# Second half's layer norm: transposing x on TensorE, or loading it already turned and spreading the scales by DMA

## Chip, cores and metric

One core of one Trainium2 chip runs the whole program. The metric is device time in microseconds, the median of the runs shown below. Engines are called as in the profile: PE (TensorE matmul), PEld (its weight load), DVE (VectorE), ACT (ScalarE), POOL (GpSimd) and SP (SyncE, which issues most transfers).

## What is computed

A transformer block on one sequence of 2048 tokens with 1024 features, in float32: an attention part and an MLP part, each behind layer norms and each added to its input.

```
x = A_x
h = x + _A_ref(_layernorm(x), wq, wk, wv, wo, beta)      # attention, 32 heads, 4 segments of 512 tokens, with a running memory
h2 = h + _B_ref(_layernorm(h), w1, b1, w2, b2)           # _B_ref normalises again, then 1024 -> 3584 -> gelu -> 1024

def _layernorm(x, axis=-1, eps=1e-5):
    m = jnp.mean(x, axis=axis, keepdims=True)
    v = jnp.var(x, axis=axis, keepdims=True)
    return (x - m) / jnp.sqrt(v + eps)
```

The change concerns the very first `_layernorm(x)`, and of it only the tokens 1024 to 2047.

## The kernel before

The tokens are worked in two halves of 1024, and a half in two slices of 512 (`sl` 0 and 1). Each half runs attention, the output product, the second layer norm, and the first MLP product (class `Mixer`). After both halves comes the second MLP product. So the first layer norm of the second half is needed when the mixer of the first half ends, and it is computed beside that mixer, in gaps.

**Precision.** Nearly every product is done three times on split operands. An operand is an upper part (`h`, a cast to the matmul type, made on ACT) and a lower part (`l`, the float32 value minus the upper part, made on DVE or POOL). `mm3` and `product` issue upper·upper, upper·lower, lower·upper. So every input of PE costs an ACT cast and a subtraction.

**Layer norm, `ln1`.** For four blocks of 128 tokens: load the block (tokens on partitions, tile `xt`), two `bn_stats` and one `bn_aggr` on DVE, three tiny operations on POOL (`v`, power, `nb`), one normalising ACT operation on 128x1024, and then eight 128x128 transposes on PE into two PSUM banks, two ACT casts (`yh`) and two DVE subtractions (`yl`). The result has features on partitions, as the q, k, v products want it. `ln1` is a generator. Each `yield` is one step, and `interleave(main, side, ratio)` runs `ratio` side steps for each main step. The four steps of one `product` are four main steps, 3 matmuls each.

**The mixer, `pair(j)`, j = 0 to 13.** It is a fast-matrix-product scheme with five products of 12 matmuls per pair. Combined weights S1 to S4 of two weight blocks (`r1`, `r2`) are added on POOL (`combine`, tiles `s`), then split by `made` (ACT cast, DVE subtraction, tiles `sa` or `sb`). For a pair j, PE runs in this order:

1. S1·T1 into `dps`,
2. S3·T3 into `bps`,
3. S2·T2 of the *next* pair into its own `bps` (`sixth(j + 1)`), whose S2 is made during this pair,
4. A22·T4, added into this pair's `bps`,
5. S4·B22, added into `dps`.

DVE drains after each: `u3` (reads `bps` after product 2), a sum with `dps`, `u2` (after product 3), and the two `ht` sums (after 4 and 5). Product 4 writes the bank that `u3` reads, so it can't start before `u3` is done. `combine(j + 2)` stands near the end of pair j in program order. In program order `made` for pair j+1 stands in pair j.

**Order.** Each engine works through its own instructions in program order. In the mixer and in attention the program order is kept by hand (`in_order`). `dps` and the transposes of `ln1` share the two PSUM banks tagged `pt`. Tiles tagged `ln` (four buffers) hold `xt`.

**Attention of the second half** starts with the products `kps`, `qps`, `vps` of unit 0 (8 steps of 3 matmuls each). `side` is there the split k and q; copied by DMA into `ks` and `qs`, they feed the first logits matmul `pqk`.

## Time and profile before

| what | value |
|---|---|
| runs | 2184.59 us median of 3 (2183.11 to 2187.11) |
| profiled execution | 2187.23 us, of which the profile's span is 2185.5 us |
| PE busy | 2157.7 us, 99% of the span |
| DVE, ACT, POOL busy | 1349.0, 1102.1, 959.7 us (62%, 50%, 44%) |
| granted clock of PE | 1.000 |
| part in question | about 710 to 880 us: mixer pairs 5 to 13 of the first half, then the first two attention units of the second |

A profile line such as `712.89 0.72 ACT L1031 ACTIVATE ht<-ht,b1c ...` reads: start in us, duration in us, engine, line of the kernel, operation, output and inputs by the program's tile names, and how many instructions were merged. In square brackets stands how long the engine sat idle before it, and what ended that. A matmul's duration overlaps that of its neighbours, since matmuls are pipelined. What a matmul costs is the distance from its start to the next start.

### The profile page before, as it was taken

How to read it: one execution, taken by the hardware profiler on the slowest of the kernel's cores; microseconds unless marked ns; L12 is line 12 of the kernel's file. 1: busy time of each engine (PE TensorE's matmuls, PEld its weight loads, DVE VectorE, ACT ScalarE, POOL GpSimd, SP SyncE). 2: the span in 40 equal slices, each digit the busy share in tenths (PEclk: the TensorE clock that was granted, in tenths of full speed). 3: DMA queues.
4: the chain of work that ended last, by engine and by line, in shares of the span. 5: the costliest groups of instructions: out<-in, count | busy, mean ns of one | idle time of the engine just before them, and what ended most of it. 6: DMA issues, size and time to landing. Idle time of an engine off the chain costs nothing.

```text
span 2185.5 us, 33210 instructions
## 1 busy us (share of the span) xinstructions
PE 2157.7 (99%) x10937; PEld 1750.4 (80%) x10937; DVE 1349.0 (62%) x2696; ACT 1102.1 (50%) x2433; POOL 959.7 (44%) x1206
## 2 busy tenths in 40 slices
PE   7999999999999999999999999999999999999999
PEld 6777777778888888877777768888887888888887
DVE  6766666665745556766667655745666665576653
ACT  5777777762543445777777752643443232322221
POOL 5534345562444434533335561534446544256330
PEclk9999999999999999999999999999999999999999
DMA  6544445664465655544444663575569865676762
GB/s 182 134 106 107 105 107 136 190 203 164 154 207 155 187 158 147 136 107 109 106 108 133 198 197 141 173 217 162 171 199 373 274 226 185 190 244 230 250 222 92
DMA packets 352405, 376.20 MB, mean 172 GB/s; under 512 B 27214, under 2 KB 244330, under 8 KB 352234
## 3 DMA queue, kind: packets, MB, share of 16 engines
q1 hardware_dynamic: 288778, 336.98, 50.7%
q10 hardware_dynamic: 63456, 37.10, 5.6%
q8 instruction: 87, 1.43, 0.3%
q14 instruction: 84, 0.69, 0.1%
HBM read 241.27 MB, written 82.38 MB: 148 GB/s over the span
## 4 chain that ended last, share of the span: by engine, by line
PE 91%; DVE 2%; DMA 2%; POOL 2%; ACT 1%; issue 1%; SPq 0%; ACTq 0%; DVEq 0%; POOLq 0%
PE po L1410 22%; PE bps L1014 10%; PE cps L1014 7%; PE dps L1014 7%; PE pst L619 4%; PE po L633 3%; PE pqk L569 3%; PE kps L127 3%; PE vps L127 3%; PE qps L127 3%; PE kps L128 3%; PE pwo L127 2%; PE kps L129 2%; PE vps L128 2%; PE pwo L129 2%; PE pwo L128 2%
## 5 line engine op out<-in xcount | busy, mean ns | idle before, releaser
L571 DVE CUSTOM_DVE_ANT_0 pqk<-pqk,mask 128x512 f32<-128x512 f32 (+2 forms) x384 | 216.9, 565 | 241.6 <-PE pqk L569 214.8
L573 ACT ACTIVATE junk<-pqk,mx 128x512 f32<-128x512 f32 (+2 forms) x384 | 225.2, 587 | 134.7 <-DVE mx L571 128.2
L626 POOL TENSOR_SCALAR_AFFINE_SELECT e<-e 128x128 f32<-128x128 f32 (+1 forms) x384 | 137.6, 359 | 268.9 <-ACT e L622 254.1
L699 POOL TENSOR_TENSOR wl<-wr,wh 128x256 fp32r<-128x256 f32 x268 | 202.1, 770 | 108.7 <-PE pqk L569 85.8
L622 ACT ACTIVATE e<-pst 128x384 f32<-128x384 f32 (+1 forms) x384 | 200.8, 529 | 70.9 <-PE pst L619 69.5
L1420 DVE TENSOR_TENSOR c<-c,po 128x512 f32<-128x512 f32 x160 | 105.4, 684 | 156.7 <-PE po L1410 153.9
L569 PE MATMUL pqk<-ks,qs 96*128 96x512 f32 (+2 forms) x384 | 138.6, 361 | 5.7 <-ACT junk L573 3.0
L619 PE MATMUL pst<-qs,ks 104*128 104x512 f32 (+3 forms) x512 | 140.9, 318 | 1.0 <-ACT e L622 0.4
L619 PEld LDWEIGHTS pst<-qs,ks 104*128 104x128 f32 x512 | 95.7, 188 | 34.7 <-ACT e L622 10.7
L1410 PE MATMUL po<-w2h,zh 128*128 128x512 f32 x378 | 120.9, 389 | 0.4 <-DVE zh L1350 0.4
L1267 POOL TENSOR_TENSOR w2r<-w2r 128x512 f32<-128x512 f32 x54 | 84.6, 1579 | 72.3 <-DMA w2r<-in_B_w 72.3
L127 PE MATMUL kps<-yh,wh 128*128 128x512 f32 (+1 forms) x264 | 113.5, 430 | 0.0
L127 PE MATMUL qps<-yh,wh 128*128 128x512 f32 x256 | 113.2, 442 | 0.0
L1014 PE MATMUL bps<-zh,sb 128*128 128x512 f32 x336 | 110.9, 391 | 0.0
L1014 PE MATMUL bps<-zh,sa 128*128 128x512 f32 x336 | 110.8, 390 | 0.0
L1126 POOL TENSOR_TENSOR s<-r 128x512 f32<-128x512 f32 x28 | 44.3, 1583 | 141.0 <-DVE sa L1142 81.3
L127 PE MATMUL vps<-yh,wh 128*128 128x512 f32 x256 | 105.0, 410 | 0.0
L1410 PE MATMUL po<-w2h,hl 128*128 128x512 f32 x322 | 103.2, 390 | 0.7 <-DVE hl L1350 0.4
L128 PE MATMUL kps<-yl,wh 128*128 128x512 f32 (+1 forms) x264 | 102.8, 389 | 0.5 <-DVE yl L165 0.4
L129 PE MATMUL kps<-yh,wl 128*128 128x512 f32 (+1 forms) x264 | 102.2, 387 | 0.0
L128 PE MATMUL qps<-yl,wh 128*128 128x512 f32 x256 | 101.0, 394 | 0.0
L128 PE MATMUL vps<-yl,wh 128*128 128x512 f32 x256 | 100.8, 394 | 0.0
(271 smaller groups left out, 6204.0 us busy)
## 6 DMA issues: line engine op xcount, KB each, us to landing
hr<-h_dram SPq DMA_DIRECT2D x112, 448.0 KB, 5.5
w2r<-in_B_w SPq DMA_DIRECT2D x122, 256.0 KB, 4.2
r<-in_B_w SPq DMA_DIRECT2D x56, 512.0 KB, 4.6
ks<-kk SPq DMA_DIRECT2D x360, 64.0 KB, 2.0
qs<-qq SPq DMA_DIRECT2D x360, 64.0 KB, 2.0
h_dram<-ht ACTq DMA_DIRECT2D x84, 256.0 KB, 3.6
wx<-in_B_w SPq DMA_DIRECT2D x56, 256.0 KB, 3.5
o_dram<-side SPq DMA_DIRECT2D x52, 256.0 KB, 4.2
```

The source lines that it names most:

```text
L127: nc.tensor.matmul(ps, ah, bh, start=first, stop=False)
L128: nc.tensor.matmul(ps, ah, bl, start=False, stop=False)
L129: acts["mm"] = nc.tensor.matmul(ps, al, bh, start=False, stop=last)
L569: nc.tensor.matmul(ps, u["qs"][0:96, j, i * P:(i + 1) * P], u["ks"][0:96, j, 0:n], start=True, stop=True)
L571: nc.vector.tensor_tensor_reduce(out=ps, in0=ps, in1=mask[:, 512 - n:512], op0=ALU.add, op1=ALU.min, scale=-SCALE, scalar=3.0e38, accum_out=m)
L573: at(now[0] + 1, lambda: nc.scalar.activation(acts["junk"][:, :n], ps, AF.Exp, bias=m, scale=-1.0, accum_out=u["mx"][:, 1, i, j:j + 1]))
L619: nc.tensor.matmul(ps[:, o:o + 512 - P * jk], u["ks"][:, j, jk * P:(jk + 1) * P], u["qs"][:, j, jk * P:512], start=True, stop=True)
L622: nc.scalar.activation(e, ps[:, :w], AF.Exp, scale=SCALE)
L626: nc.gpsimd.affine_select(d, d, pattern=[[0, 2], [1, P]] if n == 2 else [[1, P]], compare_op=ALU.is_ge, fill=0.0, base=0, channel_multipli ...
L699: nc.gpsimd.tensor_tensor(l[:, c], wr[:, c], raw(h)[:, c], op=ALU.subtract)
L1014: nc.tensor.matmul(ps, x_[:, c, :], y_[:, c, :], start=first and c == 0 and n == 0, stop=last and c == 3 and n == 2, skip_group_check=True)
L1410: nc.tensor.matmul(ps, x_[:, k], y_[k], start=opens and k == 0 and i == 0, stop=closes and k == self.KP - 1 and i == 2, skip_group_check=True)
```

## The change

The host hands the kernel a second copy of x, transposed (`A_xT`, 1024 features by 2048 tokens). A new class `Columns` replaces `ln1` for the second half:

- `load` and `stats`: as before, the token blocks are loaded and their statistics taken on DVE and POOL. The results 1/std and -mean/std of four blocks lie side by side in `rn` (128 x 8).
- `turn`, `keep`, `spread`: one PE transpose makes `rn` into 8 rows of 128, ACT copies them to `rt`, a 4 KB DMA stores them in DRAM, and a second DMA reads them back onto all 128 partitions as `rows` (128 x 2 x 512).
- `columns`: four loads of 256 features by 512 tokens of `A_xT` (tile `xc`).
- `apply`: DVE multiplies `xc` by the row of 1/std (128x1024), POOL adds the row of -mean/std (128x1024).
- `upper`, `lower`: ACT casts to `yh`, DVE subtracts to `yl`, 128x1024 each, from SBUF and not from PSUM.

All steps of both slices up to `spread` lie in the last nine mixer pairs, at hand-set steps and with ratio 0.21 in place of 0.17. The `apply` steps of slice 1 lie in attention unit 0 (before, slice 1 ran on through units 0 and 1).

```diff
+    class Columns:
+        def load(self, t):
+            self.xs[t] = lnp.tile([P, D], F32, tag="ln", name="xt", bufs=4)
+            nc.sync.dma_start(self.xs[t], x[0, r0:r0 + P, :])
...
+        def stats(self, t):
+            for i in range(2):
+                nc.vector.bn_stats(st[:, i, :], self.xs[t][:, 512 * i:512 * i + 512])
+            nc.vector.bn_aggr(mv, st)
+            r = rn[:, t:t + 1]
+            nc.gpsimd.tensor_scalar(v[:, 0:1], mv[:, 1:2], 1.0, EPS, op0=ALU.mult, op1=ALU.add)
+            nc.gpsimd.tensor_tensor(r, v[:, 0:1], mhalf, op=ALU.pow)
+            nc.gpsimd.tensor_scalar(rn[:, 4 + t:5 + t], mv[:, 0:1], -1.0, r, op0=ALU.mult, op1=ALU.mult)
+
+        def turn(self):
+            ps = psum.tile([P, 512], F32, tag="av", name="prn", bufs=1)[0:8, 0:P]
+            nc.tensor.transpose(ps, self.rn, ident)
+            self.rt = acts["rnp"].tile([P, P], F32, name="rt", bufs=1)[0:8, :]
+            nc.scalar.copy(self.rt, ps)
+
+        def keep(self):
+            nc.sync.dma_start(rn_dram[self.half, self.sl], self.rt)
+
+        def spread(self):
+            self.rows = acts["rnp"].tile([P, 2, 512], F32, name="rows", bufs=1)
+            nc.sync.dma_start(self.rows.rearrange("p a n -> p (a n)"),
+                              rn_dram[self.half, self.sl].rearrange("k p -> (k p)").partition_broadcast(P))
+
+        def columns(self, c):
+            self.ws[c] = w = lnp.tile([P, 2, 512], F32, tag="ln", name="xc", bufs=4)
+            nc.sync.dma_start(w, xt_[256 * c:256 * c + 256, t0:t0 + 512].rearrange("(c p) n -> p c n", p=P))
+
+        def apply(self, c):
+            w = self.ws[c]
+            r, nb = (self.rows[:, i, :].unsqueeze(1).to_broadcast([P, 2, 512]) for i in range(2))
+            nc.vector.tensor_tensor(w, w, r, op=ALU.mult)
+            nc.gpsimd.tensor_tensor(w, w, nb, op=ALU.add)
...
+        def upper(self, c):
+            nc.scalar.copy(self.home(0, c), self.ws[c])
+
+        def lower(self, c):
+            nc.vector.tensor_tensor(self.home(1, c), self.ws[c], raw(self.home(0, c)), op=ALU.subtract)
+
+        def columns_at(self, *steps, lag):
+            for c, m in enumerate(steps):
+                self.at(m, partial(self.apply, c))
+                self.at(m + lag, partial(self.upper, c))
+                self.at(m + lag + 1, partial(self.lower, c))
...
-            acts["ahead"] = ln1(1, 1, gap=2)
-            interleave(chain(*(mixer.pair(j) for j in range(HP - 9, HP))),
-                       chain(ln1(1, 0, 2), islice(acts["ahead"], 3)), 0.17)
+            acts["rnp"] = tc.alloc_tile_pool(name="rn1", bufs=1, reuse_waits="tile")
+            one, two = Columns(1, 0), Columns(1, 1)
+            for t in range(4):
+                one.at(0, partial(one.load, t))
+                one.at(6 + t, partial(one.columns, t))
+                two.at(20 + 2 * t, partial(two.load, t))
+                two.at(26 + 2 * t, partial(two.columns, t))
+            one.rows_at(3, 4, 5, 6, turn=9, keep=10, spread=12)
+            one.columns_at(15, 17, 19, 21, lag=3)
+            two.rows_at(23, 25, 27, 29, turn=32, keep=33, spread=35)
+            interleave(chain(*(mixer.pair(j) for j in range(HP - 9, HP))), steps(one, two), 0.21)
+            two.columns_at(1, 3, 5, 7, lag=3)
+            acts["ahead"] = steps(two)
...
+    inputs = {**inputs, "A_xT": np.asarray(inputs["A_x"])[0].T}
```

Where the instructions then stand is shown at three places. The first is POOL's order in the mixer, pairs 9 and 10. `s` are the four sums of a `combine`; the sums s_8266 to s_8269 before, and s_8271 to s_8274 now, are those that pair 10 casts. Before:

```order
L1129 TENSOR_TENSOR s_8149<-r_8053,s_8147 128x512
L1126 TENSOR_TENSOR s_8266<-r_8177 128x512
L1127 TENSOR_TENSOR s_8267<-s_8266,r_8176 128x512
L1128 TENSOR_TENSOR s_8268<-r_8176,r_8177 128x512
L1129 TENSOR_TENSOR s_8269<-r_8176,s_8267 128x512
L141 TENSOR_SCALAR v<-mv 128x1
L142 TENSOR_TENSOR v<-v,mhalf 128x1
L147 TENSOR_SCALAR nb<-mv,v 128x1
L1126 TENSOR_TENSOR s_8389<-r_8301 128x512
```

The same place now:

```order
L1217 TENSOR_TENSOR s_8158<-r_8071,s_8156 128x512
L283 TENSOR_TENSOR xc<-xc,rows 128x1024 x3
L1214 TENSOR_TENSOR s_8271<-r_8182 128x512
L1215 TENSOR_TENSOR s_8272<-s_8271,r_8181 128x512
L1216 TENSOR_TENSOR s_8273<-r_8181,r_8182 128x512
L1217 TENSOR_TENSOR s_8274<-r_8181,s_8272 128x512
L283 TENSOR_TENSOR xc<-xc,rows 128x1024
L256 TENSOR_SCALAR v<-mv 128x1
L257 TENSOR_TENSOR rn<-v,mhalf 128x1
L258 TENSOR_SCALAR rn<-mv,rn 128x1
L1214 TENSOR_TENSOR s_8396<-r_8296 128x512
```

Three 128x1024 additions of slice 0 now stand on POOL ahead of one `combine`, and a fourth with the small operations ahead of the next one.

The second place is DVE from the end of pair 9 to `u3` of pair 10 (`sa`, `sb`: lower parts of the weights; the last row of each list is `u3`). Before:

```order
L165 TENSOR_TENSOR yl_7951<-pt,yh_7950 128x4x128
L1038 TENSOR_TENSOR ht<-bps,p1r 128x512
L134 BN_STATS st<-xt 128x6 x2
L138 BN_AGGR mv<-st 128x2
L1038 TENSOR_TENSOR ht<-dps,u_8122 128x512
L1142 TENSOR_TENSOR sb<-s_8267,sb 128x512
L1142 TENSOR_TENSOR sb<-s_8266,sb 128x512
L1142 TENSOR_TENSOR sb<-s_8268,sb 128x512
L1169 TENSOR_TENSOR u_8341<-bps,p1r 128x512
```

The same place now:

```order
L294 TENSOR_TENSOR yl_8239<-xc,yh_8238 128x1024
L282 TENSOR_TENSOR xc<-xc,rows 128x1024
L1126 TENSOR_TENSOR ht<-bps,p1r 128x512
L1126 TENSOR_TENSOR ht<-dps,u_8131 128x512
L1230 TENSOR_TENSOR sb<-s_8272,sb 128x512
L1230 TENSOR_TENSOR sb<-s_8271,sb 128x512
L1230 TENSOR_TENSOR sb<-s_8273,sb 128x512
L294 TENSOR_TENSOR yl_8239<-xc,yh_8238 128x1024
L282 TENSOR_TENSOR xc<-xc,rows 128x1024
L1257 TENSOR_TENSOR u_8341<-bps,p1r 128x512
```

A `lower` and a multiply of 128x1024 now stand between the weights' lower parts and `u3`. The multiply ahead of the `ht` sums of pair 9 is the one that the third of the three POOL additions waits for.

The third place is DVE at the start of the second half's attention, from the lower part of k to that of q (`side`). Before:

```order
L440 TENSOR_TENSOR side<-kps,side 128x512
L682 CAST ks_8733<-pat 8x2048
L165 TENSOR_TENSOR yl_8801<-pt,yh_8800 128x4x128
L382 SCALAR_TENSOR_TENSOR pk,zc<-e,r 128x512
L165 TENSOR_TENSOR yl_8801<-pt,yh_8800 128x4x128
L682 CAST ks_8734<-pat 8x2048
L134 BN_STATS st<-xt 128x6 x2
L138 BN_AGGR mv<-st 128x2
L440 TENSOR_TENSOR side<-qps,side 128x512
```

The same place now:

```order
L528 TENSOR_TENSOR side<-kps,side 128x512
L770 CAST ks_8747<-pat 8x2048
L294 TENSOR_TENSOR yl_8824<-xc,yh_8823 128x1024
L282 TENSOR_TENSOR xc<-xc,rows 128x1024
L470 SCALAR_TENSOR_TENSOR pk,zc<-e,r 128x512
L770 CAST ks_8748<-pat 8x2048
L294 TENSOR_TENSOR yl_8824<-xc,yh_8823 128x1024
L282 TENSOR_TENSOR xc<-xc,rows 128x1024
L528 TENSOR_TENSOR side<-qps,side 128x512
```

Two `lower` and two multiplies of 128x1024 stand where two 128x512 subtractions and one block's statistics stood.

## Prediction

> **What bounds the kernel now.** The page first, then the waits of PE alone in the part that changes (690 to 920 us; columns: who waited for whom, us in total, times, longest).

> ```profile
> span 2185.5 us, 33210 instructions
> PE 2157.7 (99%) x10937; PEld 1750.4 (80%) x10937; DVE 1349.0 (62%) x2696; ACT 1102.1 (50%) x2433; POOL 959.7 (44%) x1206
> ...
> PE dps L1014 <- DVE ht L1038: 0.9, 1, 0.9
> PE pqk L569 <- ACT junk L573: 0.8, 1, 0.8
> ```

> PE is the bound everywhere: two waits in 230 us. So each PE instruction removed is worth its distance in PE's stream, and each new wait of PE costs its full length. Next the tile `xt` from 700 us on, and PE's timeline about one group of transposes and about the first wait.

> ```profile
> L161 PE MATMUL pt<-ident,xt x64: 270/272/273, 740.5 to 878.4; 128*128 128x128 f32 x64
> ...
> 854.89 0.39 PE L129 MATMUL vps<-yh,wl 128*128 128x512 f32 x1
> 855.12 0.60 PE L161 MATMUL pt<-ident,xt 128*128 128x128 f32 x4
> 855.47 0.48 PE L127 MATMUL kps<-yh,wh 128*128 128x512 f32 x1
> 855.78 0.39 PE L128 MATMUL kps<-yl,wh 128*128 128x512 f32 x1
> ...
> 810.35 0.39 PE L1014 MATMUL dps<-zh,sb 128*128 128x512 f32 x1
> 811.61 0.47 PE L1014 MATMUL dps<-zh,sa 128*128 128x512 f32 x1 [0.88 <-DVE ht L1038]
> ```

> A 512-column matmul keeps a distance of 0.23 (854.89 to 855.12). With a group of four transposes, the matmul after L127 starts 0.66 after 855.12 and not 0.23. A group costs 0.43, not the 1.09 that four durations of 272 ns suggest.

> Now one undisturbed mixer pair (j = 5) on DVE, ACT and POOL. Zero is the `ht` sum at 712.17; the next pair's is 13.6 later.

> ```profile
> 712.17 0.69 DVE L1038 TENSOR_TENSOR ht<-dps,u 128x512 f32<-128x512 f32 x1 [2.03 <-PE dps L1014]
> 714.71 2.99 DVE L1142 TENSOR_TENSOR sa<-s,sa 128x512 fp32r<-128x512 f32 x3 [1.85 <-ACT sa L1141]
> 717.62 0.68 DVE L1169 TENSOR_TENSOR u<-bps,p1r 128x512 f32<-128x512 f32 x1
> 720.33 0.69 DVE L1156 TENSOR_TENSOR u<-bps,p1r 128x512 f32<-128x512 f32 x1 [1.30 <-PE bps L1014]
> 725.77 0.69 DVE L1038 TENSOR_TENSOR ht<-dps,u 128x512 f32<-128x512 f32 x1 [0.59 <-DMA r<-in_B_w]
> ...
> 712.89 0.72 ACT L1031 ACTIVATE ht<-ht,b1c 128x512 f32<-128x512 f32 x1 [2.00 <-DVE ht L1038]
> 714.05 1.67 ACT L1141 CAST sa<-s 128x512 fp32r<-128x512 f32 x3 [0.44 <-ACT ht L1031]
> 719.06 0.72 ACT L1031 ACTIVATE u<-u,b1c 128x512 f32<-128x512 f32 x1 [3.34 <-DVE u L1038]
> ...
> 715.53 1.61 POOL L1126 TENSOR_TENSOR s<-r 128x512 f32<-128x512 f32 x1 [5.48 <-DVE sa L1142]
> 717.23 1.63 POOL L1127 TENSOR_TENSOR s<-s,r 128x512 f32<-128x512 f32 x1
> ```

> Offsets in the pair: gelu 0.7, casts of S2, S1, S3 from 1.9, their lower parts 2.5 to 5.5, `u3` 5.5 to 6.1, `u2` 8.2. A product is 12 matmuls, 2.72 us. `u2` starts 0.2 after its product's successor did, so product 4 starts at 8.0, and product 3 at 5.3. The slack: S2's lower part is wanted at 5.7 (third matmul) and is there by 3.5; `u3` must end by 8.0 and ends at 6.1, 1.8 spare. POOL adds S1 and S2 for the *next* pair at 3.4 to 6.7, about 9 us before ACT casts them. That lead is what holds the mixer together, and it exists since nothing stands ahead of `combine` on POOL.

> **The change part by part.** *PE.* 64 transposes go: 16 groups by 0.43 = 6.9 off. Two transposes of `rn` come: a lone one between 0 and a group's 0.43; I take 0.1 each, since four share the 0.43. The wait at 811.61 goes: `dps` found its `pt` bank still held (1.26 from start to start, less 0.23: 1.0), and no transpose takes a `pt` bank any more. The 0.8 of `pqk` on ACT I leave as it is (bounds: 0 to 1.0 off). So far -7.7.

> *New elementwise work.* The nearest rows of its size, and the statistics, which stay:

> ```profile
> L926 DVE TENSOR_TENSOR hb<-ht,b2c x16: 1172/1210/1227, 510.5 to 1377.7; 128x1024 f32<-128x1024 f32 x16
> L104 POOL TENSOR_TENSOR wl<-wr,wh x2: 2401/2406/2411, 832.9 to 835.6; 128x1024 fp32r<-128x1024 f32 x2
> 834.52 1.04 ACT L103 CAST wh<-wr 128x1024 fp32r<-128x1024 f32 x1
> 723.65 1.28 DVE L134 BATCH_NORM_STATS2 st<-xt 128x6 f32<-128x512 f32 x2
> 724.97 0.21 DVE L138 BATCH_NORM_AGGREGATE mv<-st 128x2 f32<-128x12 f32 x1
> 781.61 0.19 POOL L141 TENSOR_SCALAR v<-mv 128x1 f32<-128x1 f32 x1 [1.61 <-DVE mv L138]
> 782.54 0.27 POOL L147 TENSOR_SCALAR nb<-mv,v 128x1 f32<-128x1 f32 x1
> ```

> So a multiply or a `lower` costs DVE 1.2, an addition POOL 2.4, an `upper` ACT 1.0, a block's statistics DVE 1.4 and then POOL 1.2. On average there is room (DVE 62% busy). The order is what matters, so I walk pairs 9 to 12 by these rows and the instruction order shown above.

> - *Pair 9.* First multiply of the pair after S3's lower part, at 4.4 to 5.7 (POOL idle, so the three take 1.9); `u3` ends 6.3, still in time. gelu of u 7.0 to 7.8, 0.4 of issue, then `upper` 8.2 to 9.2 ahead of the casts of A22 and S4 (to 10.3); their lower parts end 11.0, `lower` 12.2, the third multiply 13.4. POOL's third addition runs 13.4 to 15.8, that is until 2.2 in pair 10, and only then may `combine` start: S1 to 3.5, S2 to 4.8, S3 to 6.1. It had a lead of 9 us and now comes 3 late.
> - *Pair 10.* Cast of S2 4.9 to 5.5, S1 to 6.0, an `upper` to 7.0, S3 to 7.6. On DVE S3's lower part ends 8.3, then a `lower` 9.5, a multiply 10.7, `u3` 11.4. PE loses about 1.1 at product 3 and has waited 3.4 in all (11.4 less 8.0) when product 4 starts. The pair takes 17.0. Late on DVE after that: `u2`, A22, S4 (16.1), a `lower` (17.3), a block's statistics (18.7), and POOL's 1.2 for them: the next `combine` starts at 19.9, 2.9 into pair 11.
> - *Pair 11.* S2 is summed at 5.5. ACT, with an `upper` between the two gelus, casts it at 5.8 too. S2's and S1's lower parts end 8.1, a `lower` 9.3, statistics 10.7, S3 11.4, `u3` 12.1. PE waits 4.1.
> - *Pair 12.* The same chain with no `lower` in it: `combine` from 0.7, `u3` ends 8.5, 0.5 to 0.6 late.

> Sum in the mixer +8.1. Bounds: 0 if the lead of 9 us covers it all after all, 12 if DVE is slowed by POOL throughout. I take the walk, since each link is a row and the order is fixed. Slice 0's earlier statistics, also ahead of a `combine`, fit: in the same walk `u3` of pair 7 ends at 6.5.

> *Transfers.* Eight `xc` loads of 512 KB (the `r` loads' size) come, two `rows` spreads and two 4 KB stores, all on SP's queue, and what is behind a waiting one there is the next `r`.

> ```profile
> 820.00:840.00 20.00, 20.00 (x90) 16.57 (x89) 10.05 (x17) 6.81 (x9) 6.57 (x7) 1.00 0.49 144
> ```

> The DMA engines are half idle (0.49), and a pair's `r` is wanted only by the `combine` at its end. I cost them at 0; if that cover went, `combine` would start later still. The allocation of 4.6 KB a partition I cost at 0 too.

> *Attention unit 0.* Zero is `kps`' first matmul.

> ```profile
> 836.66 0.39 PE L127 MATMUL kps<-yh,wh 128*128 128x512 f32 x1
> 854.20 0.39 PE L569 MATMUL pqk<-ks,qs 96*128 96x512 f32 x1
> ...
> 844.48 0.69 DVE L440 TENSOR_TENSOR side<-kps,side 128x512 fp32r<-128x512 f32 x1 [5.44 <-ACT side L434]
> 847.24 0.68 DVE L382 SCALAR_TENSOR_TENSOR pk<-e,r 128x512 f32<-128x512 f32 x1
> 848.55 1.22 DVE L682 CAST ks<-pat 8x2048 fp32r<-8x2048 f32 x1
> 851.24 0.64 DVE L440 TENSOR_TENSOR side<-qps,side 128x512 fp32r<-128x512 f32 x1
> ...
> 849.31 3.10 SPq L417 DMA_DIRECT2D qs<-side  x3
> DMA to landing us min/median/max: 2.0/2.2/3.7
> ```

> `pqk` has no slack today: q's lower part ends at 851.9, its copy lands 2.0 later, 853.9, and `pqk` starts at 854.2 (17.5). Without the three groups ahead of it PE is there at 16.2. DVE's chain from the lower part of k (ends 8.5) becomes 1.2 + 1.2 + 1.2 + 0.7 + 1.2 + 1.2 + 1.2 = 8.0, so q's lower part ends at 17.1, not 15.2, and lands at 19.1. PE waits 3.1 with the weight load (bounds 1.0, nothing later than today, to 4.6). The third `pqk` then waits for its bank, as DVE has two `lower` more to do first: 0.7 (0 to 1.5). Later DVE and ACT have less to do than before, but PE hardly waits there.

> Sum: -6.9 + 0.2 - 1.0 + 8.1 + 3.1 + 0.7 = +4.2. The profiled execution took 2187.2 (2185.5 of span and 1.7 around it), 2.6 above the median 2184.6. So 2191.4 for such an execution, and 2188.8 against the median.

> [...] Three lower parts took 2.99 while POOL was adding. With POOL idle:

> ```profile
> 756.48 1.90 DVE L1142 TENSOR_TENSOR sb<-s,sb 128x512 fp32r<-128x512 f32 x3 [1.85 <-ACT sb L1141]
> ```

> `u3`, which reads PSUM, kept its 0.68 beside an addition. [...] By the rows, four more such meetings (two multiplies beside POOL's weight splits at the end of the mixer, and `lower` and `pk` beside the additions in unit 0) would add 4 by 1.1 = 4.4.

> **Rivals.**
> - *The cover holds, faster.* POOL's lead would have to absorb the additions, so that `u3` stays in time. For it: 9 us of lead and DVE half idle. Against it: the third addition waits for a multiply that can't end before 13.4. Time: -7.7 and the 1.0 floor of `pqk`, 2177.9. It decides on the multiply ending by about 8 in pair 9.
> - *Only the first stall is paid*, pairs 11 and 12 recover since the statistics come earlier than walked: -7.7 + 3.4 + 1.0, 2181.3.
> - *DVE and POOL get in each other's way*, by the rows above: 2188.8 + 4.4 = 2193.2, slower.

> **How the numbers follow.** The walk 0.60 (own range 2185 to 2193), cover 0.18, first stall only 0.10, contention 0.12. About 0.2% (4.4 us) is what a measurement of this kernel can tell from no change: below 2180.2 is faster, above 2189.0 slower. The walk's centre lies at that upper edge, so it is split, a little under half above: same 0.32, slower 0.28. Faster: 0.18 + 0.02 = 0.20; same: 0.32 + 0.08 = 0.40; slower: 0.28 + 0.12 = 0.40. The range takes in both outer cases: 2177.5 to 2195.5.

> **What the next profile would show.** No L161-like transposes after 40 us but two small `prn`. New rows of PE `bps` waiting for DVE `u`, some 2 to 3 us each in pairs 10 and 11, the pairs 17 long. POOL's first sum of that `combine` following an `xc` addition. `pqk` waiting for DMA `qs` about 3 us. Wrong I would be if PE has no such rows (gain 7), or if DVE's 128x1024 rows are far from 1.2.

## The result, and the profile after

The changed kernel takes 2198.58 us (median of 6 runs, 2195.89 to 2201.0), the kernel before 2185.38 (6 runs): ratio 1.0059, 95% interval 1.0045 to 1.0073. It is 13.2 us slower. The forecast was 2188.8 in a range up to 2195.5, so the time lies beyond the range on its slow side. The profiled execution after took 2197.16 (1.4 under its median), that of before 2187.2 (1.8 over its median), so the two spans differ by only 9.9.

First the two longest entries among the waits of PE alone from 690 to 920 us, kernel after, columns as in the prediction:

```profile
PE pqk L657 <- issue: 6.9, 1, 6.9
PE bps L1102 <- DVE u L1257: 5.5, 2, 2.9
```

Two waits for `u3` in the mixer, as forecast, and one of 6.9 at the first `pqk`, where 3.1 was forecast. In the kernel after, L282 is the multiply, L283 the addition, L294 the lower part, L256 a statistic's small operation, L1214 to L1217 `combine`, L1230 the lower parts of S1 to S4, L1257 `u3`, L528 the lower parts of k and q, L770 the pattern cast, L104 and L787 the weight splits. The mixer's pair 10, whose zero is now 779.60, on the timeline of the kernel after:

```profile
779.15 2.43 POOL L283 TENSOR_TENSOR xc<-xc,rows 128x1024 f32<-128x1024 f32 x1 [5.28 <-DVE xc L282]
781.54 1.29 POOL L1214 TENSOR_TENSOR s<-r 128x512 f32<-128x512 f32 x1
...
784.89 3.41 DVE L1230 TENSOR_TENSOR sb<-s,sb 128x512 fp32r<-128x512 f32 x3 [4.62 <-ACT sb L1229]
788.23 1.21 DVE L294 TENSOR_TENSOR yl<-xc,yh 128x1024 fp32r<-128x1024 f32 x1
789.36 1.21 DVE L282 TENSOR_TENSOR xc<-xc,rows 128x1024 f32<-128x1024 f32 x1
790.50 0.68 DVE L1257 TENSOR_TENSOR u<-bps,p1r 128x512 f32<-128x512 f32 x1
```

The third addition ends 2.0 into the pair (walked: 2.2), `combine` follows at once, and `u3` ends at 11.6 (walked: 11.4). Now attention unit 0, DVE and POOL on the same timeline. `kps` starts at 841.64 (first row).

```profile
841.64 0.39 PE L127 MATMUL kps<-yh,wh 128*128 128x512 f32 x1
...
849.37 3.26 DVE L770 CAST ks<-pat 8x2048 fp32r<-8x2048 f32 x1
...
857.17 3.27 DVE L770 CAST ks<-pat 8x2048 fp32r<-8x2048 f32 x1
...
862.75 0.68 DVE L528 TENSOR_TENSOR side<-qps,side 128x512 fp32r<-128x512 f32 x1
...
837.83 6.61 POOL L104 TENSOR_TENSOR wl<-wr,wh 128x1024 fp32r<-128x1024 f32 x2 [12.41 <-DVE wh L101]
...
849.10 2.43 POOL L283 TENSOR_TENSOR xc<-xc,rows 128x1024 f32<-128x1024 f32 x1
...
856.54 2.81 POOL L283 TENSOR_TENSOR xc<-xc,rows 128x1024 f32<-128x1024 f32 x1
```

Each pattern cast, 1.22 when alone (848.55 in the kernel before), begins inside an addition and ends 1.1 after that addition does (851.53 and 852.63; 859.35 and 860.44). So its end seems to follow POOL's; `no_adds_slice1` below tests this. POOL loses as well: two weight splits of 2.4 took 6.6. The lower part of q ends at 863.43, 21.8 behind `kps` instead of the 17.1 of the prediction, and `pqk` starts 2.05 later, about what its copy takes to land (1.9 to 2.7 from issue to landing for the copies into `qs` from 855 to 870; the waits name no releaser there, only "issue"). Last, PE after that wait, and the same stretch by windows (columns as on the page, PEclk is the last but two):

```profile
865.48 0.77 PE L657 MATMUL pqk<-ks,qs 96*128 96x512 f32 x1 [6.93 <-issue]
866.05 0.63 PE L127 MATMUL vps<-yh,wh 128*128 128x512 f32 x1
866.47 0.63 PE L128 MATMUL vps<-yl,wh 128*128 128x512 f32 x1
...
873.36 0.39 PE L128 MATMUL kps<-yl,wh 128*128 128x512 f32 x1
873.59 0.40 PE L129 MATMUL kps<-yh,wl 128*128 128x512 f32 x1
```

```profile
860.00:880.00 20.00, 14.48 (x59) 11.36 (x60) 17.41 (x34) 7.23 (x17) 9.82 (x10) 0.74 0.51 135
```

Behind the wait the 512-column matmuls keep a distance of mostly 0.43 until 871.8, then mostly 0.23 again, and the granted clock of the window is 0.74. A shorter stretch of this kind follows the 2.9 us wait of pair 11 (distances of 0.40 to 0.43, a granted clock of 0.91 in the window 800 to 820). The prediction had no term for it.

### The profile page after: what moved, and what is told of

Its sections match the earlier page's. It is cut to its first block, busy times and chain, and to the rows that moved or that the text cites. A ratio compares the mean times of both kernels' runs of the same rounds, so it can differ in the third digit from the quotient of the medians.

```text
span 2195.4 us, 33111 instructions
## 1 busy us (share of the span) xinstructions
PE 2156.9 (98%) x10875; PEld 1745.1 (79%) x10875; DVE 1375.5 (63%) x2696; ACT 1092.4 (50%) x2419; POOL 979.2 (45%) x1214
## 4 chain that ended last, share of the span: by engine, by line
PE 88%; DVE 3%; POOL 3%; DMA 2%; issue 2%; ACT 1%; SPq 0%; ACTq 0%; POOLq 0%; DVEq 0%
PE po L1498 21%; PE bps L1102 9%; PE cps L1102 7%; PE dps L1102 6%; PE pst L707 3%; PE po L721 3%; PE pqk L657 3%; PE kps L127 3%; PE kps L128 3%; PE kps L129 3%; PE qps L127 3%; PE vps L127 2%; PE pwo L127 2%; PE pwo L129 2%; PE pwo L128 2%; PE qps L128 2%
## 5 line engine op out<-in xcount | busy, mean ns | idle before, releaser
L787 POOL TENSOR_TENSOR wl<-wr,wh 128x256 fp32r<-128x256 f32 x268 | 203.9, 777 | 108.9 <-PE pqk L657 92.9
L657 PE MATMUL pqk<-ks,qs 96*128 96x512 f32 (+2 forms) x384 | 139.3, 363 | 12.7 <-issue 6.9
L127 PE MATMUL kps<-yh,wh 128*128 128x512 f32 (+1 forms) x264 | 114.0, 432 | 0.0
L127 PE MATMUL qps<-yh,wh 128*128 128x512 f32 x256 | 112.9, 441 | 0.0
L127 PE MATMUL vps<-yh,wh 128*128 128x512 f32 x256 | 104.9, 410 | 0.0
L128 PE MATMUL kps<-yl,wh 128*128 128x512 f32 (+1 forms) x264 | 103.0, 390 | 0.5 <-DVE yl L165 0.4
L1214 POOL TENSOR_TENSOR s<-r 128x512 f32<-128x512 f32 x28 | 42.7, 1525 | 135.2 <-DVE sa L1230 61.1
L129 PE MATMUL kps<-yh,wl 128*128 128x512 f32 (+1 forms) x264 | 102.9, 390 | 0.0
L128 PE MATMUL vps<-yl,wh 128*128 128x512 f32 x256 | 101.1, 395 | 0.0
L128 PE MATMUL qps<-yl,wh 128*128 128x512 f32 x256 | 100.9, 394 | 0.0
```

What stands on the lines that cost most here:

```text
L127: nc.tensor.matmul(ps, ah, bh, start=first, stop=False)
L128: nc.tensor.matmul(ps, ah, bl, start=False, stop=False)
L129: acts["mm"] = nc.tensor.matmul(ps, al, bh, start=False, stop=last)
L657: nc.tensor.matmul(ps, u["qs"][0:96, j, i * P:(i + 1) * P], u["ks"][0:96, j, 0:n], start=True, stop=True)
L787: nc.gpsimd.tensor_tensor(l[:, c], wr[:, c], raw(h)[:, c], op=ALU.subtract)
```

## The experiments

Each run is set against runs of the kernel before on the same chip and in the same hour; ratios are to those, since the median of before moved between 2185.2 and 2186.5 from one set of runs to the next. The theories at the outset: (1) in the mixer it is the order on POOL, additions ahead of `combine`; (2) in unit 0 it is POOL and DVE holding each other up; (3) or it is simply the amount of work on DVE.

### Unit 0: is it POOL, or the number of DVE operations?

`no_adds_slice1` leaves out slice 1's additions and nothing else:

```
  nc.vector.tensor_tensor(w, w, r, op=ALU.mult)
+ if not self.sl:
      nc.gpsimd.tensor_tensor(w, w, nb, op=ALU.add)
```

> Leaves out slice 1's four additions on POOL (its mean is then not taken off); every DVE instruction stays where it is. If DVE waits for POOL's additions in unit 0, the casts of the pattern fall from 3.26 to 1.22, the lower parts to 1.2, q's lower part ends about 16.5 after kps' first matmul instead of 21.8, and the first pqk waits 2 instead of 6.9, with no slow stretch of 2.8 behind it: 2198.6 - 4.9 - 2.8 = 2190.9. If the number of DVE instructions ahead of q's lower part is what counts, the wait stays above 5: 2196 or more.

Measured: 2191.73 us, ratio 1.0028 (1.0018 to 1.0038). The DVE timeline of this kernel (`kps` at 843.41):

```profile
851.05 1.22 DVE L771 CAST ks<-pat 8x2048 fp32r<-8x2048 f32 x1
...
855.62 1.22 DVE L771 CAST ks<-pat 8x2048 fp32r<-8x2048 f32 x1
...
859.15 0.68 DVE L529 TENSOR_TENSOR side<-qps,side 128x512 fp32r<-128x512 f32 x1
```

The same DVE instructions in the same order, and the casts are 1.22 again. The lower part of q ends 16.4 behind `kps`, PE waits 2.2 for its copy and no slow stretch follows. That is theory (2), and within a microsecond of its numbers; by (3) nothing should have changed.

`before_two_adds` is the converse: the kernel before with two additions on POOL that nobody needs.

```
  ...                                # a tile dm of 128 x 2 x 512 is allocated
+ at(2, lambda: nc.gpsimd.memset(dm, 0.0))
+ for _ in range(2):
+     at(11, lambda: nc.gpsimd.tensor_tensor(dm, dm, dm, op=ALU.add))
```

> The kernel before, with two additions of 128x1024 on POOL (each 2.4 us, on a tile that nothing else uses) put in attention unit 0 behind v's weight split. Nothing waits for them but POOL's later small operations. If DVE's casts and operations with two SBUF inputs wait for POOL's additions, the second pattern cast (1.22 us, at 11.9 behind kps) takes 2.5 to 3.5 or the operations ahead of it do, q's lower part ends 1.5 to 3 later than 15.2, and the first pqk starts 1.5 to 3 later than 17.5 behind kps. Rival: the durations stay as they are, and pqk starts at 17.5.

Measured, in one profiled execution:

```profile
847.91 2.21 DVE L682 CAST ks<-pat 8x2048 fp32r<-8x2048 f32 x1
...
854.33 0.47 PE L569 MATMUL pqk<-ks,qs 96*128 96x512 f32 x1 [1.70 <-DMA qs<-side]
```

The second cast took 2.21 (1.22 before; a little less than the 2.5 expected) and again ended 1.1 after the addition beside it, which ended at 849.04; `pk` took 1.66 (0.68), the lower part of q ended 17.3 behind `kps` (15.2), and PE waited 1.7 for its copy, `pqk` starting 1.9 later. The execution as a whole was not longer (2184.48), within what single executions of before differ by, so this run speaks for the mechanism and not for its price.

`slice1_unit1` moves the pieces out of the way instead:

```
- two.columns_at(1, 3, 5, 7, lag=3)
+ two.columns_at(11, 13, 15, 17, lag=3)
```

> Slice 1's column pieces move ten steps (1, 3, 5, 7 to 11, 13, 15, 17), behind q's lower part of attention unit 0. If the multiplies, additions and lower parts there make the first pqk wait, its 6.9 us fall to 1 or less, and the slow stretch of PE behind it (about 2.8 us) goes too: 2198.6 - 5.9 - 2.8 = 2190, less by up to 3 us of new waits in units 0 and 1. The mixer's waits (7.2) stay. Rival: the pieces only move the wait along, to the later pqk or to kk and qq of unit 1: 2196 or more.

Measured: 2203.46, ratio 1.0085 (1.0072 to 1.0097), slower still. The first `pqk` waits 0.2, as expected, but the waits of PE in this kernel from 690 to 920 now read

```profile
PE bps L1102 <- DVE u L1257: 5.5, 2, 2.8
PE pqk L657 <- ACT junk L661: 3.8, 2, 3.6
PE pqk L657 <- DMA qs<-qq: 3.7, 1, 3.7
PE pq L667 <- ACT junk L661: 3.4, 1, 3.4
```

with slow stretches (distances of 0.43) behind the three long waits of attention. The rival was right for the price: the pieces took the waits along. One other place was tried; whether attention has a better one stays open.

### The mixer: order on POOL, or DVE ahead of `u3`?

`one_step_later` shifts two pieces by one step, so that the third addition follows `combine`:

```
- one.columns_at(15, 17, 19, 21, lag=3)
+ one.columns_at(15, 17, 20, 22, lag=3)
```

> Only the third and fourth column pieces of slice 0 move one step (19, 21 to 20, 22), so that POOL's third addition is issued behind the mixer's four sums (combine) of that pair and not ahead of them. The same instructions run. If the order on POOL makes the waits of PE in pairs 10 and 11 (2.6 and 2.9 us for u, about 7.2 in all) and the gate's slow stretch after them (1.7), these go: kps' first matmul near 833 instead of 841.6, and the time 2198.6 - 8.9 = 2189.7. The first pqk still waits about 6.9, since nothing changes behind kps. Rival: the waits come from the amount of work on DVE and POOL, wherever it stands: then less than 2 us is won, 2197 or more.

Measured: 2196.34, ratio 1.0051 (1.0039 to 1.0063), only 2.2 under the kernel after. `combine` did come back early (772.91 instead of 781.54), yet PE still waited 3.0 in pair 10:

```profile
785.15 2.75 POOL L283 TENSOR_TENSOR xc<-xc,rows 128x1024 f32<-128x1024 f32 x1 [5.02 <-DVE xc L282]
...
785.60 3.39 DVE L294 TENSOR_TENSOR yl<-xc,yh 128x1024 fp32r<-128x1024 f32 x1
788.91 0.68 DVE L1257 TENSOR_TENSOR u<-bps,p1r 128x512 f32<-128x512 f32 x1
```

The new lower part, 1.22 alone, stands ahead of `u3` and ends 1.1 after the addition (788.99 and 787.90). In pairs 11 and 12 PE waited another 1.7 and 1.4 for `u3`. So mending the order of this one addition was not enough: wide work on DVE ahead of `u3` makes PE wait as well.

`no_apply` asks what is left without the wide work:

```
- self.at(m, partial(self.apply, c))
+ self.at(m, lambda: None)
```

> Leaves out the multiplies and the additions (the output is then not normalised); loads, statistics, the turned scales, their spread, the upper and lower parts stay. This is the floor of the change: 16 groups of transposes by 0.43 and the bank wait of 1.0 gone, two small transposes more: 2185.4 - 7.7 = 2177.7, or 2178.7 with the first pqk waiting 1. If the loads and spreads on SP's queue cost anything, or the statistics ahead of combine do, it is above 2180, and PE shows waits in the mixer.

Measured: 2183.99, ratio 0.9991 (0.9983 to 1.0), six above the floor that the sum had. PE waits 2.9 and 1.4 for `u3`. POOL shows why: slice 1's first statistic waits for DVE, and `combine` behind it.

```profile
794.25 0.19 POOL L256 TENSOR_SCALAR v<-mv 128x1 f32<-128x1 f32 x1 [14.81 <-DVE mv L253]
...
795.40 1.30 POOL L1214 TENSOR_TENSOR s<-r 128x512 f32<-128x512 f32 x1
```

POOL idles 14.8 us ahead of an operation of 0.19. So three small operations that wait for DVE can take `combine`'s lead as well as an addition of 2.4 can.

`behind_sums` therefore issues all of slice 0's additions and slice 1's statistics behind `combine`, and `no_apply_behind` does so without the wide work.

```
  ...                                # slice 1's loads move along
- one.columns_at(15, 17, 19, 21, lag=3)
+ one.columns_at(16, 17, 20, 21, lag=3)
- two.rows_at(23, 25, 27, 29, turn=32, keep=33, spread=35)
+ two.rows_at(24, 25, 28, 29, turn=32, keep=33, spread=35)
```

> The kernel without multiplies and additions still waited 2.9 and 1.4 us for u3 in two pairs: there POOL's small operations on a statistic of slice 1, which wait for DVE, stood ahead of combine. So the theory is now: whatever stands ahead of combine on POOL and waits for a DVE instruction late in its pair takes combine's lead of 9 us. Here every addition and every statistic of slice 1 is issued behind the combine of its pair (slice 0's pieces at 16, 17, 20, 21, slice 1's statistics at 24, 25, 28, 29). Expected: combine's first sum starts within 7 us of its pair's zero again, PE waits at most 2 us in the mixer in place of 7.2 and no slow stretch there: 2198.6 - 5.2 - 1.7 = 2191.7, kps near 835. The first pqk still waits 6.9. Rival: DVE's own load ahead of u3 (a lower part, a multiply, statistics) is enough: PE waits 4 or more in the mixer, 2195 or more.

Measured: 2198.0, ratio 1.0058 (1.0045 to 1.0071), no gain. PE waits 1.5 and 4.6 for `u3`, because two pieces now stand close together and the second multiply meets the first addition (3.44 for a multiply of 1.22). The rival was right on the time: DVE's work ahead of `u3`, drawn out by POOL, was enough.

> Leaves out multiplies and additions (output not normalised), with the steps of behind_sums. If the statistics ahead of combine were what the kernel without them still paid (4.3 us of waits), this is the floor: 2184.0 - 4.3 - 1.4 = 2178.3, with no wait of PE over 1 us from 690 to 860. Rival: the loads or DVE's lower parts make u3 late: 2182 or more.

Measured: 2182.05, ratio 0.9983 (0.9975 to 0.9992); the profiled execution had a span of 2179.4 and two waits for `u3`, 1.7 and 1.4. Better than `no_apply`, but the time is the rival's (2182 or more) and the bound of 1 us per wait was missed. Lower parts and statistics still stand ahead of `u3` there; which of them makes the wait was not tested.

`adds_on_dve` takes POOL out by giving DVE the additions:

```
- nc.gpsimd.tensor_tensor(w, w, nb, op=ALU.add)
+ nc.vector.tensor_tensor(w, w, nb, op=ALU.add)
```

> All eight additions run on DVE instead of POOL (about 1.2 us each instead of 2.4), so DVE gets more work and POOL gets none of the layer norm's wide work. If DVE loses time to POOL's additions by waiting for them (casts of 3.26 instead of 1.22), then in unit 0 the chain from k's lower part to q's takes 11.7 us by the rows, against 14.8 now, and the wait of the first pqk falls from 6.9 to 3.8, though two more additions stand in it. In the mixer, combine is on time again, and DVE's u3 comes at most 1 us late: PE waits 0 to 2 in place of 7.2, no slow stretch. Sum: 2198.6 - 6.2 - 1.7 - 3.1 - 1 = 2186.6. Rival: DVE's instructions count by their number, not by POOL: pqk waits 9 and u3 comes 1.2 later still in each pair, 2200 or more.

Measured: 2201.54, ratio 1.0071 (1.0059 to 1.0084). In unit 0 the durations were as expected, casts of 1.50 and 1.22, the lower part of q at 19.2; PE waited 5.0 (3.8 expected). In the mixer PE waited 2.8, 3.6 and 2.9 for `u3`, where at most 2 in all had been expected: POOL has nothing wide there any more, and DVE alone is late. So theory (3) has a share in the mixer. In unit 0 it does not account for the 6.9, since there the wait fell although DVE had two operations more.

### The slow stretches

`before_waits` makes PE wait on purpose, in the kernel before, by computing `u3` of pairs 0 to 4 several times over (the numbers are what comes on top of the first).

```
- nc.vector.tensor_tensor(u3, bps, p1, op=ALU.add)
+ for _ in range(1 + acts.get("late", {}).get(j, 0)):   # 5, 7, 9, 11, 6
+     nc.vector.tensor_tensor(u3, bps, p1, op=ALU.add)
```

> The kernel before, with u3 of the mixer's first five pairs computed 6, 8, 10, 12 and 7 times over (0.6 us more each, the same result, read from PSUM), so that PE has to wait about 1.1, 2.3, 3.5, 4.7 and 1.7 us ahead of product 4. If a wait of PE of more than about 2.6 us is followed by a slow stretch, the 512-column matmuls behind the 3.5 and 4.7 keep a distance of 0.43 in place of 0.23 for some 3 to 4 us (1.5 to 2 us each), and those behind 1.1, 1.7 and 2.3 keep 0.23. If the wait's length is not what counts, slow stretches stand elsewhere or nowhere.

Measured, in one profiled execution: waits of 1.7, 3.2, 4.6, 6.1 and 2.4. Their PE rows:

```profile
669.63 0.50 PE L1014 MATMUL bps<-zh,sb 128*128 128x512 f32 x1 [3.21 <-DVE u L1170]
669.97 0.40 PE L1014 MATMUL bps<-zl,sb 128*128 128x512 f32 x1
...
688.15 0.66 PE L1014 MATMUL bps<-zh,sa 128*128 128x512 f32 x1 [4.60 <-DVE u L1170]
688.61 0.63 PE L1014 MATMUL bps<-zl,sa 128*128 128x512 f32 x1
```

Behind 3.2 nothing is slow, behind 4.6 a stretch of 3.6 us is, behind 6.1 one of 5.9, but behind 2.4 one of 3.5 too. So a wait can bring the stretch on, and between 2.1 and 3.8 its length alone does not say whether; the expected bound of 2.6 does not hold. Over all profiles here (630 to 930 us), all 7 waits of 4.6 and more were followed by one, 13 of 20 between 2.1 and 3.8, and 1 of 21 between 1.0 and 1.8. The shortest waits with a stretch behind them were 1.6 (`one_per_pair`) and 2.2 (`by_slots`). The expectation of `one_step_later` calls such a stretch the gate's; what the traces show of it are the distances of 0.43 in place of 0.23 and the lower granted clock (0.74 above), and not what sets it off beyond the wait ahead of it.

### A version without the waits

By these runs, what stands in a pair should keep off three things: `combine` on POOL, the stretch of DVE ahead of `u3`, and another piece's addition. Nine pairs have no room for that with one piece to a pair, and `ah1`, where slice 1's result goes, is held by the mixer until its end. `one_per_pair` starts with the mixer's first pair, puts at most one piece into a pair, and does slice 1's multiplies and additions in the mixer too, leaving only its upper and lower parts for unit 0.

```
  ...                                # loads and slice 0's statistics move as well
- interleave(chain(*(mixer.pair(j) for j in range(HP - 9, HP))), steps(one, two), 0.21)
- two.columns_at(1, 3, 5, 7, lag=3)
+ one.columns_at(16, 20, 24, 28, lag=3)
+ two.rows_at(24, 28, 32, 37, turn=39, keep=40, spread=41)
+ for c in range(4):
+     two.at((45, 49, 53, 57)[c], partial(two.apply, c))
+ interleave(chain(*(mixer.pair(j) for j in range(HP - 14, HP))), steps(one, two), 0.21)
+ for c in range(4):
+     two.at(1 + 2 * c, partial(two.upper, c))
+     two.at(2 + 2 * c, partial(two.lower, c))
```

> All of the layer norm's steps start with the mixer's first pair instead of the sixth, at most one multiply and addition per pair, each behind combine, and slice 1's multiplies and additions run in the mixer too; only its upper and lower parts are left in attention unit 0. All of the work is done. If order and DVE-POOL contention are the whole cost, PE waits 0 to 2 us in the mixer and at most 1 us at the first pqk: 2178 to 2181. Rival: eight additions of 2.4 us beside DVE's lower parts slow every pair, or new loads delay r: 2187 or more.

Measured: 2193.74, ratio 1.0041 (1.0029 to 1.0054). The pairs tell more than the sum (here and below from `ht` sum to `ht` sum on DVE, as in the prediction): those with slice 1's additions took 13.6 to 13.8, those with slice 0's up to 18.2. The mixer's first pair has four chunks (of 3 matmuls) more than the others, and 0.21 gives 4.2 steps to a pair, so the pieces drift. Slice 0's first two additions fell behind `combine`, the other two, each with a statistic, ahead of it: `combine` then started 1.8 into the next pair, and these two pairs took 18.2 and 17.3. But slice 1's additions fell ahead of `combine` too, which started up to 1.3 into the next pair (808.67 and 823.50, pairs from 808.65 and 822.25), and those pairs took 13.6 and 14.4. So the order alone does not cost. What sets the dear pairs apart is that `combine` started later in them, and that a lower part and a statistic stood in them as well; which of the two counts was not separated. `by_slots` puts exactly four steps into a pair:

```
  ...                                # loads and slice 0's statistics move as well
- interleave(chain(*(mixer.pair(j) for j in range(HP - 14, HP))), steps(one, two), 0.21)
+ interleave(chain(iter([None] * 4), *(mixer.pair(j) for j in range(HP))), steps(one, two), 0.2000001)
- two.rows_at(24, 28, 32, 37, turn=39, keep=40, spread=41)
+ two.rows_at(23, 27, 31, 35, turn=38, keep=39, spread=40)
-     two.at((45, 49, 53, 57)[c], partial(two.apply, c))
+     two.at((44, 48, 52, 53)[c], partial(two.apply, c))
```

> As one_per_pair, but the steps now fall on four fixed places in every pair (one step every 5 chunks of 12 matmuls are 3): multiply, addition and lower part directly behind combine, the upper part behind u3, a statistic behind u3, nothing of it between S3's lower part and u3; slice 1's last additions in the last pair, which has no combine behind it. In one_per_pair only the three pairs with this order (slice 1's additions) kept 13.6 us, the others took 14.2 to 18.2. If order is what counts, all pairs stay within 0.5 of 13.6, kps comes at 831 to 833, the first pqk waits about 1: 2178 to 2181. Rival: the additions beside DVE's lower parts cost wherever they stand: pairs of 14.5 and more with an addition, 2186 or more.

Measured: 2183.3, ratio 0.9984 (0.9975 to 0.9994), about 15 under the kernel after, and faster than before, by little. Pairs with slice 1's additions took 13.6 to 13.8, with slice 0's 14.6, 16.5, 16.4 and 14.1, so the rival held for slice 0's pairs, though not for the time. PE waits 1.0 and 2.2 in the mixer. `by_slots_late` moves slice 1's lower parts in unit 0:

```
-     two.at(2 + 2 * c, partial(two.lower, c))
+     two.at((10, 11, 13, 14)[c], partial(two.lower, c))
```

> As by_slots, with slice 1's four lower parts behind q's lower part of attention unit 0 (steps 10, 11, 13, 14 instead of 2, 4, 6, 8). If the lower parts ahead of q's make the first pqk wait its last 1 us, that goes, about 1 faster than by_slots; rival: they then delay the reads of pqk's banks by as much, same time as by_slots.

Measured: 2185.5, ratio 0.9996 (0.9987 to 1.0005), no gain. The first `pqk` had no wait left in `by_slots`; now the third waits 1.5 for its bank, which is what the rival said.

What was left in slice 0's pairs were slice 1's statistics, whose small POOL operations again stood ahead of `combine`, which so ran beside DVE's lower parts. `by_slots_small` issues them one step later (`small` is the second half of `stats`), for which `mv` gets a fourth buffer; `by_slots_lower` also moves the lower part away from the multiply.

```
- mv = lnp.tile([P, 2], F32, name="mv", bufs=3)     # and the same in ln_scale
+ mv = lnp.tile([P, 2], F32, name="mv", bufs=4)
  self.at(m, partial(self.stats, t))
+ self.at(m + (m % 4 == 3), partial(self.small, t))
```

```
  ...                                # slice 1's loads move along
- one.columns_at(16, 20, 24, 28, lag=3)
+ for c in range(4):
+     one.at(16 + 4 * c, partial(one.apply, c))
+     one.at(17 + 4 * c, partial(one.upper, c))
+     one.at(19 + 4 * c, partial(one.lower, c))
- two.rows_at(23, 27, 31, 35, turn=38, keep=39, spread=40)
+ two.rows_at(24, 28, 32, 35, turn=38, keep=39, spread=40)
```

> As by_slots, but a statistic's three small POOL operations are issued one step later, behind combine, while its DVE part stays behind u3. If they are what delays combine in the pairs with slice 0's additions, combine starts within 5 us of the pair's zero again, A22's and S4's lower parts fall from 1.7 to 0.7 and the multiply from 2.31 to 1.2, those pairs (14.6, 16.5, 16.4, 14.1) take 14.6 at most, and the time is 3 to 4 less than by_slots: 2179.5. Rival: the pairs stay at 16 since DVE has too much ahead of the pair's last sum, 2183.

Measured: 2185.09, ratio 0.9995 (0.9986 to 1.0004).

> As by_slots_small, and slice 0's lower parts stand behind u3 instead of ahead of the next multiply, its upper parts behind S1's cast, slice 1's first statistics beside the multiply. If the two operations in a row are what is left, the pairs with additions take 13.6 to 14.0 and the time is 2177 to 2178.5. Rival: the upper parts delay S3's cast, or the lower parts beside combine are held up, and u3 or u2 comes late: 2180 or more.

Measured: 2185.83, ratio 0.9996 (0.9987 to 1.0005). The mechanism held: the pairs took 14.5, 14.5, 13.4 and 12.7 in the first, `kps` started at 833.95, and PE had a single wait of 0.6 between 690 and 920, none of it in the mixer. Between `by_slots` and `by_slots_small` DVE keeps its order; on POOL only the place of the small operations differs, so it was they that cost the waits of 1.0 and 2.2. In the second the pairs took 14.7, 14.7, 12.7 and 13.1, not the 13.6 to 14.0 expected; PE had no wait in the mixer either. Yet neither was faster than before, for the products with `sb` had become slow everywhere, 13.9 for a pair without any piece. Groups by line of `by_slots_small`, and below of `by_slots_small_3`, which differs in one number only (columns: ns minimum, median, maximum):

```
- mv = lnp.tile([P, 2], F32, name="mv", bufs=4)     # and the same in ln_scale
+ mv = lnp.tile([P, 2], F32, name="mv", bufs=3)
```

```profile
L1107 PE MATMUL bps<-zh,sb x336: 392/395/477, 648.5 to 1638.6; 128*128 128x512 f32 x168
L1107 PE MATMUL dps<-zh,sb x224: 392/395/397, 656.8 to 1641.4; 128*128 128x512 f32 x112
```

```profile
L1107 PE MATMUL bps<-zh,sb x336: 389/389/478, 649.1 to 1633.5; 128*128 128x512 f32 x168
L1107 PE MATMUL dps<-zh,sb x224: 389/389/389, 657.3 to 1636.2; 128*128 128x512 f32 x112
```

> by_slots_small with three buffers of mv instead of four, so that the weights' pool starts 8 bytes a partition earlier; the instructions and their order are the same. If the place of the weights in SBUF made the products with sb slow, they fall from 395 to 389 ns again, undisturbed pairs from 13.92 and 13.70 to 13.60, and as this holds for both halves' 28 pairs, the time falls by 28 x 0.2 = 5.6 to 2179.5. Rival: the slower products come from something else (the order on POOL, the extra step): 2185 as before.

Measured: 2177.23, ratio 0.995 (0.9936 to 0.9963), 2.3 under what was expected.

> by_slots_lower with three buffers of mv instead of four, else the same. By the same reason 5.6 less than 2185.8: 2180.2, and the pairs with additions 0.2 to 0.3 shorter than the 13.7 to 14.7 that they took. Rival: no change, 2185.8.

Measured: 2179.51, ratio 0.9961 (0.9949 to 0.9974). The time is as expected, though the pairs with additions stayed at 14.7. Both are faster than before, and `by_slots_small_3` is the fastest kernel here: 9.3 us under the kernel before on its chip and some 21 under the kernel after. From start to start on PE every pair of its mixer takes 13.6, or 13.8 with a `prn`. Its timeline on PE at unit 0:

```profile
831.65 0.39 PE L127 MATMUL kps<-yh,wh 128*128 128x512 f32 x1
...
848.31 0.47 PE L662 MATMUL pqk<-ks,qs 96*128 96x512 f32 x1 [0.40 <-PE vps L129]
```

## Why the prediction was wrong, step by step

`by_slots_small_3`, which has none of these waits, gives the terms apart. Its profiled span is 2176.1, against 2185.5 before and 2195.4 after. Ahead of the mixer the three do the same, but reach its first product at 640.94, 641.25 and 640.30; these offsets are no part of the change.

- *The transposes, the bank wait, `rn`: forecast -7.7, measured -9.4* (2176.1 less 2185.5; the medians differ by 9.3). The step was right, somewhat small. On PE pairs of the kernel before with one group of transposes take 14.09 and a pair with two 14.57, where pairs with none take 13.60: a group costs 0.49 there and not 0.43, which makes 0.9 over the 16. Another 0.3 is the offset; the last 0.5 I have not followed.
- *The mixer: forecast +8.1, measured +10.6* (from its first product to `kps` 201.3 against 190.7; the starts of `kps` alone, 841.64 and 831.65, give 10.0, as the kernel after began 0.6 earlier). The walk was right in kind and close in number: third addition until 2.0 (2.2), `u3` of pair 10 at 11.6 (11.4). When product 4 started, PE had lost 3.9 in pair 10 (3.4) and 4.8 in pair 11 (4.1); 3.0 and 4.0 of this are shown as waits, the rest is wider distances beside them. Pair 12 lost 0.3 (0.6). Behind the wait of pair 11 nine matmuls took about 0.41 each in place of 0.23. That is 1.6, which the sum left out.
- *The first `pqk`: forecast +3.1, measured +7.2* (23.84 behind `kps` against 16.66). This is the step that failed. The chain "1.2 + 1.2 + 1.2 + 0.7 + 1.2 + 1.2 + 1.2" took its durations from rows of before, where POOL was idle for 5.9 at that place, and the change itself fills POOL there without a break. With POOL's additions away the chain ended at 16.4, with them at 21.8. The prediction had the effect in its rows (three lower parts 2.99 beside POOL's additions, 1.90 without), priced it at 1.1 for each meeting by them, and put it among the rivals at 4.4 with a chance of 0.12. Two of its four meetings, 2.2, lay in unit 0, where 4.1 more than walked was lost; the two at the end of the mixer cost PE nothing, the last pair taking 10.9 in all three kernels. Its list of meetings left out the two casts, which have one SBUF input; each lost 2.0 (3.26 and 3.27 in place of 1.22). The rows show how much: 3.26 is what was left of the addition (2.16), and 1.1. Nor is 1.1 the price of every meeting: beside POOL's weight splits in unit 0 a lower part took 1.65 and a multiply 1.76, beside an addition in `behind_sums` a multiply took 3.44, all of them 1.22 alone.
- *The stretch behind that wait: not in the sum, measured +2.1* (from the first `pqk` to the end 1329.9 against 1327.8). Thirteen matmuls by 0.2 give 2.6. The 2.1 itself is uncertain: before and `before_two_adds`, which do the same work from there on, differ by 3.0 in it.
- *The third `pqk`'s bank: forecast +0.7, measured 0.* The late first `pqk` probably gave DVE the time it needed; no run tests this.

Together -9.4 + 10.6 + 7.2 + 2.1 - 0.6 (the earlier start) = +9.9, the difference of the spans. The rival *cover holds* fell with the third multiply, which ended 13.3 into pair 9 and not by about 8. *Only the first stall* fell with pair 11. *Contention* had the sign and the place in unit 0, and about half the price. As to what makes the mixer's waits, the prediction's walk rests on one link above all (`combine` behind an addition); the runs show three: operations on POOL ahead of `combine` that wait for DVE, wide DVE operations ahead of `u3`, and the meeting of two pieces. None of them has a price of its own: by `one_per_pair` the first costs little where the pair has slack left.

## What to carry to other kernels

Take a duration from the trace only together with what the neighbours did at the time: a chain of DVE casts and two-input operations has to be priced again once the change fills POOL beside it (here casts of 1.22 took up to 3.27 beside an addition, a multiply of 1.22 took 3.44). Before adding work to an engine that "has room on average", list which instruction of the next stage stands behind it in that queue, and how many microseconds of lead that one lives on; here moving three operations of 0.2 to 0.6 us behind it took the last waits out of the mixer. And to a wait of the bounding engine add the stretch at about half the rate that may follow it (here 0.43 between matmuls in place of 0.23, behind 13 of 20 waits between 2.1 and 3.8 and all 7 of 4.6 and more).
